# First batch of an attention and snake-MLP kernel: last keys in 1 KB rows on VectorE, three warm-up products fewer, two main products first, last division on GpSimd

## The chip, the cores and the metric

The kernel runs on one core of a Trainium2 chip. The metric is the device time of one execution in microseconds; the time of a kernel is the median of its runs. Engines are named as in the profile: PE is TensorE (PEld its weight loads), DVE is VectorE, ACT is ScalarE, POOL is GpSimd, and SP is the engine that issues most DMAs.

## The reference, cut to what matters

The first part is attention with pooled keys and values: batch 8, 8 heads, 576 tokens, head dimension 64. Keys and values are means over 8 neighbouring tokens, so that 72 keys are left.

```python
k_p = k.reshape(B, H, Sp, pool, D).mean(axis=3)        # pool 8, Sp 72
v_p = v.reshape(B, H, Sp, pool, D).mean(axis=3)
scores = scale * np.matmul(q, k_p.transpose(0, 1, 3, 2))
scores = scores - np.max(scores, axis=-1, keepdims=True)
attn = np.exp(scores)
attn = attn / (np.sum(attn, axis=-1, keepdims=True) + 1e-09)
out = np.matmul(attn, v_p)
```

Its output, 4608 tokens of 512 features, is the input of a second part, which is most of the work:

```python
h = x @ w_in                       # 512 -> 2048
s = np.sin(alpha * h)
g = h + s * s / (alpha + 1e-09)
y = g @ w_out                      # 2048 -> 512
```

All is float32.

## The kernel before

**Stages.** Tokens are worked on in nine units of 512 (`hidden(u, extra)`), each with four groups J of hidden features. A group's product is made by a scheme of the Strassen kind with seven products of half blocks, in the order 1, 5, 6, 2, 7, 3, 4. A unit thus has 28 slots, one product to a slot (L765, eight matmul records). The operands `as...` (combinations of blocks of `w_in`) are made by `combine_w_in` (L636); the operands `bt` (combinations of blocks of x) by `sums_of_x` (L738). After each product small pieces of work follow in the next slot: copies of partial sums on ScalarE (L791, L803, L805), sines and squares (L771, L778), additions on VectorE (L744, L832), a store of g to DRAM (L839). The second product of the MLP follows at the end (L1084); nothing in the change touches it.

**Attention beside it.** `carry(u)` writes out by hand in which slot of unit u the attention work for a later batch stands (`at(slot, f, ...)`). The order on every engine is the order in which the program issues the work; a DMA on SP likewise. So an instruction that waits holds back all that stands behind it on its engine.

**The first batch** has nothing to hide behind. `first_batch` runs it by pairs of heads: `load_k_heads` loads 512 of the 576 tokens' keys in rows of four tokens, adds them in two steps (L161, L163), and `k_head` sums pairs of rows by a matmul with `twos` (a matrix that adds neighbouring rows, L353) and copies the keys to `kb2` (L354). The last 64 tokens of all heads (8 keys each) are loaded by `load_k_rest` as 64 rows of 2 KB, added in three steps on GpSimd (L148) and transposed by `k_last` (L359, copied at L360). `q_head` transposes queries (L370, copied at L371). `products_head` multiplies the pair's queries with the keys (L391), and its keys include the last ones. `soft_shift` subtracts the maximum on VectorE (L397, L399), `soft_exp` takes the exponential on ScalarE (L405), `norm_head` sums (L411), takes the reciprocal (L412) and multiplies (L417). `a_head` transposes the attention weights of two pairs (L445, L453; copied at L447, L454), `values` multiplies them with pooled v (L533, L535), and `to_x` writes x (L504). Before k arrives, `warm` issues matmuls on the identity matrix, whose results nobody reads (L866). `refine` is a step that improves `c`, a square root (L605, L606).

Pairs 0 and 1 (heads 0 to 3) are finished in `first_batch`. Heads 4 to 7 go on in `carry(0)`: `a_head(1)` in slot 1, ahead of the second product of the slot order, `values` in slot 2, then the last 64 queries of batch 0: `rest_q` (L378, L379), `score(4)` (L320, L327, L328), `exp(4)` in slot 9, `norm_rest` in slot 20 (L423, L424, L428, L432, all on VectorE), `a_rest` in slot 23 (L460, L461, L462), `values_rest` in slot 24 (L546, L548).

Batch 1's attention runs in the same unit: `exp` and `norm` of four tiles (L336; sums L342, L343 on VectorE, multiplication L344 on GpSimd), `turn` (L470 and the lines after it), `move` (16 DMAs from `tr` to `aM`, L490), `all_values` in slot 26 (L563, L576; a one-element copy at L570, named `order`, reads the second bank in between), then `turn_q` (L210), which uses `tr` again. `load_v` of batch 1 sums v on GpSimd (L120), `load_k(2, e)` loads batch 2's keys in slot 16 (L108) and sums them there too (L120).

Of the kernel before, what the change touches and what calls it, by code (L numbers as in the profile page):

```python
# [13 lines left out]
F32 = mybir.dt.float32  # L14
AX = mybir.AxisListType.X
AF = mybir.ActivationFunctionType
OP = mybir.AluOpType
PSUM = bass.MemoryType.PSUM

P = 128  # L20
POOL = 8
# [19 lines left out]
class Kernel:  # L41
# [102 lines left out]
    def load_k_rest(self, x, out):  # L144

        D = self.D
        self.nc.sync.dma_start(out=x, in_=self.k[0, :, 4 * P:, :].rearrange("h (k t) d -> h k (t d)", t=POOL))
        add = lambda o, w, both=lambda y: y: self.nc.gpsimd.tensor_tensor(out=o, in0=both(x[:, 0:w]), in1=both(x[:, w:2 * w]), op=OP.add)  # L148
        add(x[:, 0:4 * D], 4 * D)
        add(x[:, 0:2 * D], 2 * D)  # L150
        add(out.rearrange("p (u d) -> p u d", u=2), D, lambda y: y.unsqueeze(1).to_broadcast([64, 2, D]))
        self.k_rest = out

# [75 lines left out]
    def attention(self, b):  # L229

        nc, D, H, Sp, NP, S = self.nc, self.D, self.H, self.Sp, self.NP, self.S
# [117 lines left out]
        def k_head(hp):  # L349

            ps = self.psum([P, 2, 64], 7 if hp % 2 else 0)
            for e in range(2):
                nc.tensor.matmul(ps[:, e], self.k_sums[:, 2 * hp + e].rearrange("p u d -> p (u d)"), self.twos[:], start=True, stop=True)  # L353
            nc.scalar.copy(out=self.kb2[:, 2 * hp:2 * hp + 2, 0:64], in_=ps)  # L354

        def k_last():

            ps = self.psum([P, H, Sp - 64], 4)
            nc.tensor.transpose(ps.rearrange("p h k -> p (h k)"), self.k_rest, self.ident[:64, :64])  # L359
            nc.scalar.copy(out=self.kb2[:, :, 64:Sp], in_=ps)  # L360
# [58 lines left out]
        def norm_rest():  # L419

            n = 64
            sm = self.sm.tile([P, H], F32, name="sm")
            nc.vector.tensor_reduce(out=sm[:n], in_=ex[:n, 5, :, 0:Sp + 1], axis=AX, op=OP.add)  # L423
            nc.vector.reciprocal(out=sm[:n], in_=sm[:n])  # L424
            for g in range(2):
                h = slice(4 * g, 4 * g + 4)
                m = sm[:n, h].rearrange("p (s e) -> p s e", s=2).unsqueeze(3).to_broadcast([n, 2, 2, 64])
                nc.vector.tensor_tensor(out=self.a4[:, 2 * g:2 * g + 2].rearrange("p e s k -> p s e k"),  # L428
                                        in0=ex[:n, 5, h, 0:64].rearrange("p (s e) k -> p s e k", s=2), in1=m, op=OP.mult)
            x = ex[:n, 5, :, 64:Sp].rearrange("p (hp e) k -> p hp e k", e=2)  # L430
            m = sm[:n].rearrange("p (hp e) -> p hp e", e=2).unsqueeze(3)
            nc.vector.tensor_tensor(out=self.z4[:, :, 0:2, :], in0=x, in1=m.to_broadcast([n, NP, 2, Sp - 64]), op=OP.mult)  # L432
# [120 lines left out]
        def all_values():  # L553
# [16 lines left out]
            nc.vector.tensor_copy(out=self.sm.tile([P, 1], F32, name="order")[:], in_=rest[:, 1, 0:1])  # L570
# [3 lines left out]
            for hp in hps:  # L574
                w, x = main[hp][1]
# [274 lines left out]
    def first_batch(self):  # L850
# [29 lines left out]
        self.load_k_rest(h[1][:64, 576:1088], far[1][:64, 1024:1152])  # L880
# [3 lines left out]
        for f in add_k[1:]:  # L884
            f()
        refine()
# [5 lines left out]
        warm(6, 3)  # L892
# [3 lines left out]
        A.q_head(1)  # L896
        A.products_head(0)
        A.k_head(1)
        A.soft_shift(0)
        A.q_head(2)  # L900
# [8 lines left out]
        A.norm_head(1, nc.gpsimd)  # L909
# [10 lines left out]
        A.norm_head(3, nc.vector)  # L920
# [10 lines left out]
    def carry(self, u):  # L931
# [5 lines left out]
        if u == 0:  # L937
            A0, A = self.att[:2]
            at(1, A0.a_head, 1, (5, 6, 7))
            at(1, self.half_k)  # L940
            at(2, A0.values, (2, 3), (2, 1))
            at(2, self.sums_of_x, 0, 1)
            at(2, A0.rest_q)
# [24 lines left out]
            at(20, A0.norm_rest)  # L968
# [9 lines left out]
            for e in range(2):  # L978
                at(16, self.load_k, 2, e)
# [348 lines left out]
```

## Time and profile before

| what | value |
|---|---|
| median of 4 runs | 923.27 us |
| the four runs | 919.65, 920.77, 925.77, 925.87 us |
| the profiled execution, its time | 920.77 us |
| its span in the profile | 919.0 us |
| its mean granted TensorE clock | 0.996 |
| TensorE busy from 0 to 6 us | 4.31 us |
| from 6 to 10 us | 2.95 of 4.00 us |
| from 10 to 15 us | 4.64 of 5.00 us |
| from 15 to 22 us | 6.18 of 7.00 us |
| from 22 to 60 us | 36.77 of 38.00 us |
| from 60 to 110 us | 48.18 of 50.00 us |
| first product L765 begins | 21.96 us |

How to read the profile: busy times are those of one execution, in microseconds from the span's start. A line such as L765 is a line of the kernel before. In a timeline a row is a run of like instructions: start, time, engine, line, operation, written tile and read tiles, count, and in brackets how long the engine stood idle before it and what it waited for. When several things were waited for, the one named is that which came last by the profile. The chain of waits follows what ended last back to the start.

### The profile page before, as it was taken

The page shows a single profiled execution, that of the slowest core. Times are in us where ns is not written, and L with a number is a line of the kernel's source. Part 1 is how long each engine was busy: PE and PEld are TensorE (multiplying, and loading weights), DVE is VectorE, ACT ScalarE, POOL GpSimd, SP SyncE. Part 2 cuts the span into 40 slices and gives each one's busy share as a digit, 9 for nine tenths or more (in the row PEclk, how much of TensorE's full clock was granted, in tenths as well). Part 3 has the DMA queues.
Part 4 walks back from the last instruction along what each step waited for, and adds up shares of the span by engine and source line. Part 5 has one row for each costly group of instructions (what it writes and reads, how often), then busy time and mean ns, then how long its engine had stood idle before and what let it go on. Part 6 is the DMA issues. An engine that isn't in the chain of part 4 may idle for free.

```text
span 919.0 us, 17718 instructions
## 1 busy us (share of the span) xinstructions
PE 903.3 (98%) x7006; PEld 819.9 (89%) x7006; DVE 670.9 (73%) x1005; ACT 435.8 (47%) x998; POOL 159.4 (17%) x155
## 2 busy tenths in 40 slices
PE   8999999999999999999999999999999999999997
PEld 6787887887878878888888899999999999999997
DVE  7666666746667566673466889988888888979894
ACT  5595685866757667586886631111111112111111
POOL 4593250612507034040000000000000000000000
PEclk9999999999999999999999999999999999999999
DMA  9984666766667556627327237171617253433401
GB/s 253 244 246 136 186 172 176 222 179 186 186 167 212 174 148 179 189 89 259 142 92 246 92 105 226 34 225 27 219 40 188 72 170 90 159 100 122 137 14 39
DMA packets 134666, 141.12 MB, mean 154 GB/s; under 512 B 49832, under 2 KB 103096, under 8 KB 134584
## 3 DMA queue, kind: packets, MB, share of 16 engines
q1 hardware_dynamic: 133240, 138.54, 52.1%
q10 hardware_dynamic: 1344, 1.45, 0.6%
q8 instruction: 55, 0.90, 0.4%
q14 instruction: 27, 0.22, 0.1%
HBM read 75.37 MB, written 47.19 MB: 133 GB/s over the span
## 4 chain that ended last, share of the span: by engine, by line
PE 90%; DMA 3%; POOL 2%; SPq 2%; DVE 1%; issue 1%; ACT 0%; POOLq 0%; ACTq 0%
PE PS L765 44%; PE PS L1084 41%; PE PS L287 2%; PE PS L563 2%; DMA a<-in_moe_w_in_dram 2%; SPq L630 1%; DMA kvin<-in_v_dram 1%; PE PS L576 1%; POOL as L636 1%; DMA home<-in_k_dram 1%; POOL ex L344 0%; POOL kvin L120 0%; DVE last L428 0%; SPq L96 0%; POOL a L636 0%
## 5 line engine op out<-in xcount | busy, mean ns | idle before, releaser
L765 PE MATMUL PS<-home,a 128*128 128x256 f32 x1152 | 264.3, 381 | 0.8 <-ACT home L504 0.5
L765 PEld LDWEIGHTS PS<-home,a 128*128 128x128 f32 x1152 | 216.5, 190 | 37.0 <-issue 4.5
L765 PE MATMUL PS<-home,as 128*128 128x256 f32 x864 | 202.7, 384 | 0.5 <-issue 0.5
L765 PEld LDWEIGHTS PS<-home,as 128*128 128x128 f32 x864 | 164.2, 192 | 24.6 <-issue 1.7
L1084 PE MATMUL PS<-s,wb 128*128 128x144 f32 x896 | 119.3, 286 | 0.4 <-ACT PS L1197 0.4
L1084 PEld LDWEIGHTS PS<-s,wb 128*128 128x128 f32 x896 | 113.7, 190 | 0.7 <-ACT PS L1197 0.6
L778 ACT ACTIVATE s<-s,c 128x256 f32<-128x256 f32 (+1 forms) x216 | 110.0, 572 | 0.0
L744 DVE TENSOR_TENSOR h<-PS,p 128x512 f32<-128x512 f32 x72 | 49.2, 684 | 79.3 <-PE PS L765 47.5
L120 POOL TENSOR_TENSOR kvin<-kvin 96x768 f32<-96x768 f32 (+3 forms) x40 | 66.3, 1659 | 194.5 <-DMA kvin<-in_v_dram 189.4
L771 ACT ACTIVATE s<-h,al 128x256 f32<-128x256 f32 x144 | 65.1, 503 | 56.1 <-DVE h L744 55.2
L1197 ACT COPY PS<-PS 128x144 f32<-128x144 f32 x56 | 14.7, 263 | 145.7 <-PE PS L1084 144.3
L771 ACT ACTIVATE s<-PS,al 128x256 f32<-128x256 f32 x144 | 59.9, 467 | 37.0 <-PE PS L765 17.4
L1084 PE MATMUL PS<-r,wb 128*128 128x144 f32 x512 | 73.2, 286 | 0.0
L1084 PE MATMUL PS<-s,a 128*128 128x144 f32 x512 | 73.2, 286 | 0.0
L832 DVE TENSOR_TENSOR h<-PS,s 128x512 f32<-128x512 f32 x36 | 24.7, 685 | 58.4 <-ACT s L778 58.4
L1084 PEld LDWEIGHTS PS<-r,wb 128*128 128x128 f32 x512 | 67.1, 190 | 0.1
L1084 PEld LDWEIGHTS PS<-s,a 128*128 128x128 f32 x512 | 67.1, 190 | 0.0
L1216 ACT COPY PS<-PS 128x144 f32<-128x144 f32 x56 | 14.7, 263 | 88.5 <-PE PS L1084 88.5
L1084 PE MATMUL PS<-s,we 128*128 128x144 f32 x384 | 54.9, 286 | 0.0
L1084 PE MATMUL PS<-x,wb 128*128 128x144 f32 x384 | 54.9, 286 | 0.0
L1084 PEld LDWEIGHTS PS<-s,we 128*128 128x128 f32 x384 | 50.4, 190 | 0.1
L832 DVE TENSOR_TENSOR h<-h,s 128x1024 f32<-128x1024 f32 x36 | 50.4, 1400 | 0.0
(185 smaller groups left out, 1191.8 us busy)
## 6 DMA issues: line engine op xcount, KB each, us to landing
g_bridge<-h SPq DMA_DIRECT2D x72, 512.0 KB
r<-g_bridge SPq DMA_DIRECT2D x31, 1152.0 KB
out_dram<-o SPq DMA_DIRECT2D x128, 72.0 KB
kvin<-in_k_dram SPq DMA_DIRECT2D x14, 576.0 KB
q<-in_q_dram SPq DMA_DIRECT2D x7, 1024.0 KB
kvin<-in_v_dram SPq DMA_DIRECT2D x14, 512.0 KB
aM<-tr SPq DMA_DIRECT2D x56, 92.0 KB
aM<-tr SPq DMA_DIRECT2D x56, 88.0 KB
```

The costliest lines, as they stand in the source:

```text
L120: self.nc.gpsimd.tensor_tensor(out=t[..., 0:w] if w > D else out, in0=t[..., 0:w], in1=t[..., w:2 * w], op=OP.add)
L287: nc.tensor.matmul(ps[e][r0 + r:r0 + r + q.shape[-1], h, :], q[s], kb[s, hp, :], start=True, stop=True)
L563: nc.tensor.matmul(o[r:r + 64], w, x, start=start and i < 2, stop=False, skip_group_check=True)
L576: nc.tensor.matmul(ps[hp], w.rearrange("p e d -> p (e d)"), x, start=False, stop=True, skip_group_check=True)
L744: add = lambda o, x, y: nc.vector.tensor_tensor(out=o, in0=x, in1=y, op=OP.add)
L765: nc.tensor.matmul(ps[:, jj, :], self.A[p][:, kk, f * P:(f + 1) * P], x[:, kk, :], start=(start and jj == 0 and kk == 0), stop=(kk == 1), ...
L771: nc.scalar.activation(out=G.s[:, i, jj, j, :], in_=src[:, jj], func=AF.Sin, scale=self.al[:, f:f + 1])
L778: nc.scalar.activation(out=x, in_=x, func=AF.Square, scale=self.c[:, f:f + 1])
L832: add = lambda o, x, y: self.nc.vector.tensor_tensor(out=o, in0=x, in1=y, op=OP.add)
L1084: nc.tensor.matmul(out, W[:, J // 2, J % 2, :], A[:, J, :], start=(start and J == 0), stop=(J == self.NJ - 1), skip_group_check=True)
L1197: nc.scalar.copy(out=x1[:, 0, :], in_=x0[:, 1, :])
L1216: nc.scalar.copy(out=x1[:, 1, :], in_=x1[:, 0, :])
```

## The change

Nine edits, all in the work of the first batch or in unit 0:

- `load_k_rest` loads the last keys as 128 rows of 1 KB (four tokens each) and no longer as 64 of 2 KB; its additions are two, on VectorE, and are issued by a function that it returns. `k_last` then sums pairs of rows by a matmul with `twos` where it transposed.
- The copy of the first pair's keys to `kb2` and that of the last keys go from ScalarE to VectorE.
- `warm(6, 3)` becomes `warm(3, 3)`.
- The additions of pairs 1 to 3's keys are issued after `k_last`; `q_head(1)` after `k_head(1)`; `refine` after the first `soft_shift`.
- `norm_head(1)` multiplies on VectorE, `norm_head(3)` on GpSimd, each the other way before.
- In `carry(0)`, `a_head(1)` goes from slot 1 to slot 2, behind `rest_q`, which itself goes to the head of slot 2; so the second product comes ahead of both.
- `norm_rest` goes from slot 20 to slot 17 and multiplies on GpSimd.
- `order` of batch 1 goes from VectorE to ScalarE.
- `load_k(2, e)` goes from slot 16 to slot 17.

```diff
-        self.nc.sync.dma_start(out=x, in_=self.k[0, :, 4 * P:, :].rearrange("h (k t) d -> h k (t d)", t=POOL))
-        add = lambda o, w, both=lambda y: y: self.nc.gpsimd.tensor_tensor(out=o, in0=both(x[:, 0:w]), in1=both(x[:, w:2 * w]), op=OP.add)
-        add(x[:, 0:4 * D], 4 * D)
-        add(x[:, 0:2 * D], 2 * D)
-        add(out.rearrange("p (u d) -> p u d", u=2), D, lambda y: y.unsqueeze(1).to_broadcast([64, 2, D]))
+        self.nc.sync.dma_start(out=x, in_=self.k[0, :, 4 * P:, :].rearrange("h (r t) d -> h r (t d)", t=4))
         self.k_rest = out
+
+        def add():
+            self.nc.vector.tensor_tensor(out=x[:, 0:2 * D], in0=x[:, 0:2 * D], in1=x[:, 2 * D:4 * D], op=OP.add)
+            both = lambda y: y.unsqueeze(1).to_broadcast([P, 2, D])
+            self.nc.vector.tensor_tensor(out=out.rearrange("p (u d) -> p u d", u=2), in0=both(x[:, 0:D]), in1=both(x[:, D:2 * D]), op=OP.add)
+        return add
...
-            nc.scalar.copy(out=self.kb2[:, 2 * hp:2 * hp + 2, 0:64], in_=ps)
+            (nc.scalar.copy if hp else nc.vector.tensor_copy)(out=self.kb2[:, 2 * hp:2 * hp + 2, 0:64], in_=ps)
...
-            nc.tensor.transpose(ps.rearrange("p h k -> p (h k)"), self.k_rest, self.ident[:64, :64])
-            nc.scalar.copy(out=self.kb2[:, :, 64:Sp], in_=ps)
+            nc.tensor.matmul(ps.rearrange("p h k -> p (h k)"), self.k_rest, self.twos[:], start=True, stop=True)
+            nc.vector.tensor_copy(out=self.kb2[:, :, 64:Sp], in_=ps)
...
-                nc.vector.tensor_tensor(out=self.a4[:, 2 * g:2 * g + 2].rearrange("p e s k -> p s e k"),
+                nc.gpsimd.tensor_tensor(out=self.a4[:, 2 * g:2 * g + 2].rearrange("p e s k -> p s e k"),
...
-            nc.vector.tensor_tensor(out=self.z4[:, :, 0:2, :], in0=x, in1=m.to_broadcast([n, NP, 2, Sp - 64]), op=OP.mult)
+            nc.gpsimd.tensor_tensor(out=self.z4[:, :, 0:2, :], in0=x, in1=m.to_broadcast([n, NP, 2, Sp - 64]), op=OP.mult)
...
-            nc.vector.tensor_copy(out=self.sm.tile([P, 1], F32, name="order")[:], in_=rest[:, 1, 0:1])
+            (nc.vector.tensor_copy if b > 1 else nc.scalar.copy)(out=self.sm.tile([P, 1], F32, name="order")[:], in_=rest[:, 1, 0:1])
...
-        self.load_k_rest(h[1][:64, 576:1088], far[1][:64, 1024:1152])
+        add_rest = self.load_k_rest(h[1][:, 576:832], far[1][:, 1024:1152])
...
-        for f in add_k[1:]:
-            f()
-        refine()
+        add_rest()
...
-        warm(6, 3)
+        warm(3, 3)
         A.k_head(0)
         A.q_head(0)
         A.k_last()
-        A.q_head(1)
+        for f in add_k[1:]:
+            f()
         A.products_head(0)
         A.k_head(1)
+        A.q_head(1)
         A.soft_shift(0)
+        refine()
...
-        A.norm_head(1, nc.gpsimd)
+        A.norm_head(1, nc.vector)
...
-        A.norm_head(3, nc.vector)
+        A.norm_head(3, nc.gpsimd)
...
-            at(1, A0.a_head, 1, (5, 6, 7))
-            at(1, self.half_k)
+            at(2, A0.rest_q)
+            at(2, A0.a_head, 1, (5, 6, 7))
+            at(2, self.half_k)
             at(2, A0.values, (2, 3), (2, 1))
             at(2, self.sums_of_x, 0, 1)
-            at(2, A0.rest_q)
...
-            at(20, A0.norm_rest)
+            at(17, A0.norm_rest)
...
-                at(16, self.load_k, 2, e)
+                at(17, self.load_k, 2, e)
```

On every engine the number of instructions stays nearly the same: TensorE has three warm-up matmuls fewer, ScalarE one copy fewer, GpSimd three additions fewer and three multiplications more.

## The prediction

> **What bounds the kernel now.** I read the page first (busy shares and the chain of waits), then granted clock by stretch, then the timeline around the edits.
>
> ```profile
> PE 903.3 (98%) x7006; PEld 819.9 (89%) x7006; DVE 670.9 (73%) x1005; ACT 435.8 (47%) x998; POOL 159.4 (17%) x155
> ...
> PE 90%; DMA 3%; POOL 2%; SPq 2%; DVE 1%; issue 1%; ACT 0%; POOLq 0%; ACTq 0%
> ```
>
> TensorE is the bound: it is busy for 98% of the span, and it does not lose work (three warm-up products apart). So the change can only win what TensorE loses in the first 90 us, which is all that it touches. Busy time by stretch from 0 to 110 us adds up to 103.0 of 110, so 7 us of idle time, and the clock adds to it:
>
> ```profile
> 27.00:30.50 3.50, 2.46 (x17) 0.75 (x17) 2.99 (x2) 1.35 (x3) 3.34 (x5) 1.00 1.15 230
> 30.50:34.00 3.50, 3.50 (x22) 2.91 (x23) 2.74 (x7) 2.32 (x5) 0.21 (x1) 0.53 1.11 344
> 75.00:78.30 3.30, 2.11 (x11) 1.31 (x10) 3.30 (x5) 2.05 (x5) 2.35 (x3) 1.00 0.63 148
> 78.30:81.70 3.40, 3.40 (x28) 2.25 (x26) 1.02 (x1) 0.66 (x3) 0.00 (x0) 0.53 0.63 148
> ```
>
> Columns: stretch, its length, busy time of TensorE, its weight loads, VectorE, ScalarE and GpSimd, granted clock, DMA share, GB/s. Each half-clock stretch follows one in which TensorE idled for over a microsecond. Eight matmuls of L765 take 3.27 and 3.18 us there and 1.9 us elsewhere, so such a stretch costs up to half its 3.4 us, 1.7 us.
>
> The first idle time is the wait of L320 for `q_rest`'s copy (1.0 us), which stands on ScalarE behind L504. The second is the division of the last tokens:
>
> ```profile
> 68.79 0.71 DVE L470 STREAM_TRANSPOSE tr<-ex 128x512 f32<-128x512 f32 x1 [1.15 <-POOL ex L344]
> 69.43 0.27 DVE L473 STREAM_TRANSPOSE tr<-ex 128x128 f32<-128x128 f32 x1
> 69.62 0.65 DVE L744 TENSOR_TENSOR h<-PS,p 128x512 f32<-128x512 f32 x1
> ...
> 70.33 3.32 PEld L765 LDWEIGHTS PS<-home,a 128*128 128x128 f32 x16 [0.17 <-DVE h L744]
> ...
> 72.95 0.74 DVE L423 TENSOR_REDUCE sm<-ex 64x8 f32<-64x584 f32 x1
> ...
> 73.84 2.94 POOL L120 TENSOR_TENSOR kvin<-kvin 96x768 f32<-96x768 f32 x2
> 73.95 3.10 DVE L428 TENSOR_TENSOR last<-ex,sm 64x256 f32<-64x256 f32 x2
> ...
> 77.12 0.34 PE L460 MATMUL PS<-ident,last 64*128 64x64 f32 x2 [0.80 <-DVE last L428]
> ```
>
> Two things are to be seen. The divisions L428 take 1.55 us each, for half the elements of the 128x512 addition L744 at 0.65 us: they run only as GpSimd's L120 lets them. And TensorE at 70.33 waits for L744, which stands on VectorE behind a transpose that waits for GpSimd's L344. GpSimd's work before it runs nearly without a gap from 46.63, when v of batch 1 has landed. So TensorE has a gate at 70.3 whose time comes from DMA and GpSimd: what is gained before it is lost there.
>
> **What the Trainium skill says.** "TensorE: Matmul & The Clock Gate", section "What's actually happening": an activity monitor gates TensorE to half clock after an idle window of about 3.4 us. The trace agrees in size (0.53 in both stretches), but here a window two thirds busy was enough. "GPSIMD Engine Reference", section "Specifications": GpSimd shares its SBUF interfaces with VectorE, and instructions of VectorE with two SBUF inputs contend. L428 agrees: 1.55 us each beside L120. The same page, "Performance versus the Vector engine": elementwise work is about twice as slow on GpSimd. It agrees: L161 128x256 takes 0.74 us on POOL and 0.39 us on DVE.
>
> **The change part by part.**
>
> *Last keys.* Removed: three L148 on POOL (0.72 + 0.59 + 0.52 = 1.83 us, from 6.51 to 8.50), which L359 waited for (1.1 us), and two ScalarE copies (0.27 + 0.21). Added on VectorE: two 128x128 additions, not in the trace as such; bounds 0.17 us each (L605, 128x16) and 0.42 us (L163, 128x256); I take 0.55 us for both, and 0.45 us for two PSUM copies (ScalarE's took 0.27 and 0.21). Same 128 KB and place in SP's queue, so I keep the landing at 6.5 us; 1 KB rows instead of 2 KB ones may move it by 0.3 us either way. The last keys are then transposed near 7.1 instead of 8.55 and the first L391 starts near 7.65 instead of 9.34. Behind the waiting addition on VectorE stand the copy of keys 0 and 1 and the sums of keys 2 and 3 (landed 7.16, now 7.57): k_head(1) runs at about 8.6, not 10.0. But q_head(1) now follows it, and the second L391 needs that copy: about 10.45 instead of 11.03. Of 1.7 us, 0.6 is left. GpSimd's sums of keys 4 to 7 gain at most 0.27 us, since L161 waits for DMA already.
>
> *Warm-ups.* Three of six matmuls (half of 2.93 us) go. k_head(0) starts when its sums are ready (4.99) instead of 6.0; nothing follows from it, since the last keys come at 7.1. Bounds: 0, or 1.7 us lost on a chain with slack if the clock falls.
>
> *Order on VectorE.* `refine` (four L605/L606: 0.17 to 0.58 us each, 0.9 to 1.4 in all) goes behind the first soft_shift, ahead of the second, and its products of two SBUF tiles meet GpSimd's sums. The second shift starts at about 11.6 (11.9 before). Division 1 moves to VectorE (L417 there: 0.97 us for both parts) and division 3 to GpSimd (1.29 us). So a_head(0) may start near 15.95 (16.86), but shift 2 waits for the division: 16.1 (15.14), and shift 3 ends near 19.4 (18.29). ScalarE's queue passes this on:
>
> ```profile
> 18.51 0.70 ACT L405 ACTIVATE ex<-ex 128x576 f32<-128x576 f32 x1
> ...
> 19.09 0.57 ACT L454 COPY aM<-PS 64x512 f32<-64x512 f32 x1
> ...
> 20.36 1.13 PE L535 MATMUL PS<-aM,vz 32*128 32x512 f32 x4
> ```
>
> Exponential 3 stands ahead of the copy L454 that L535 needs. Later by 1.1 us, it puts the first main product at about 22.6 instead of 21.95: 0.65 us lost; bounds 0.9 gained to 1 lost.
>
> *Second main product first.* Before, from the start F of the first L765: a_head(1) to F+3.2, second product to F+5.0, values to F+7.1, the last tokens' queries, the wait, scores to F+9.6, third product at F+9.55. After: two products to F+3.9, queries 4.3, a_head(1) 5.9, values 8.35 (their copies are no longer covered by the product: 0.2), scores 9.1, while two L504 (1.08) and L738 (0.69) still stand before the third product: F+10.25. It loses 0.7 us, wins the L320 wait, and leaves about 1.2 us idle elsewhere. If the half clock after it goes, 1.7 us come back. So TensorE comes out between 1.7 us earlier and 1.4 us later. To the gate at 70.3 an earlier arrival counts nothing.
>
> *Division of the last tokens.* L423 and L424 (0.74 + 0.19) now stand between L473 and L744, so the gate opens at 71.3: 0.95 us lost. GpSimd does L428 and L432 behind L344: 0.55 + 0.55 + 0.26 by L417's rate there, from 70.65 to 72.05. L460 needs them at 76.8: hidden, with 4.7 us of cover. Gone are the waits around L460 (between products it took TensorE 2.07 us, from 75.78 to 77.85; without waits about 0.6, as the four like transposes of L378 took 0.46: 1.45 us) and probably the half clock behind them (1.7). TensorE reaches all_values at about 83.55 instead of 85.75. There the next comes late: the aM moves of L490 (16 issues, 10.1 us on SP) start after the last transpose, now 72.6 instead of 71.8, and their landing, 83.4 before by VectorE's wait in L210, becomes 84.2. So some 1.6 us are kept, 2.2 at best. k of batch 2 is issued behind a store (2.26 us of SP, 10 us later), summed 1.7 us later and needed at 91: covered. `order` on ScalarE (0.16 us) keeps TensorE from L210's queue, which now ends near 87.4.
>
> **Sum.** -1.45 -1.7 +0.95 of the division gives -2.2, of which late moves leave -1.6; the front adds 0, since up to 0.9 us of delay hides in the later gate. The profiled execution (span 919.0, 920.77 around it) would go to 919.2; on the median of four runs (923.27) it is **921.6**.
>
> **Rivals.** *Larger gain:* the gate itself opens earlier. GpSimd's additions are stretched where VectorE reads two SBUF tiles (one L636 2.30 us instead of 1.27, another 1.92); shifted in time they may lose up to 2 us, and with 2.2 kept the gain is 4.2: 919. Against it: GpSimd starts from the same landing of v.
>
> *Slower:* the half clock comes back after the new stall. The idle 0.95 us at 70.4 and the 1.2 us before the third product fill a window as the old waits did. One more half-clock stretch (1.7), with the old ones kept and 0.5 us of front delay beyond the gate, gives +2.2: 925.5. It decides once a window drops to about two thirds busy; for it speaks that such windows were throttled twice, against it that 6 to 10 us, with 2.95 of 4.00 busy, was not.
>
> *Nothing:* the aM moves land as late as the gain is large: 923.3.
>
> **Chances.** Forecast 0.48, larger gain 0.2, slower 0.24, nothing 0.08. The four runs shown lie from 919.65 to 925.87, and this spread comes on top of every case: range 917.3 to 926.0. One per cent is 9.2 us, about what a measurement here tells from no change; all idle and half-clock time of the front is 10 us, so faster by more has 0.03; slower by more would need five more half-clock stretches: 0.03.
>
> **What would show it.** Right: VectorE's divisions gone near 74 to 77.6, L460 without wait, a wait of about 1 us for L744's line near 70.4, full clock from 78 to 82, a first main product at 22 to 23. Wrong: a third half-clock stretch, TensorE waiting near 84 for far longer than 1 us, or a first L391 not before 9.

## The result, and the profile after

| what | before | after |
|---|---|---|
| median of all runs | 919.71 us (56 runs, 914.50 to 930.67) | 919.84 us (35 runs, 915.64 to 927.83) |
| ratio after to before | | 1.0004, 95% interval 0.9991 to 1.0018 |
| profiled execution, its time | 920.77 us | 921.34 us |
| its span | 919.0 us | 919.5 us |
| its mean granted clock | 0.996 | 0.998 |

No difference can be measured: the interval reaches from 0.8 us faster to 1.7 us slower. The ratio is taken from the fast runs alone, without the few that lie more than 1.5% above their kernel's fastest, and so it is not the quotient of the two medians. From L148 on, line numbers of after are those of before plus two for what the text speaks of (L765 is L767, L391 is L393, L490 is L492); in e3a and e7 it is plus four, in e9 and e10 plus two.

The page, its busy shares and the end of its chain of waits:

```profile
PE 902.6 (98%) x7001; PEld 819.8 (89%) x7001; DVE 666.2 (72%) x1005; ACT 435.4 (47%) x997; POOL 162.2 (18%) x155
...
PE 94%; DVE 2%; DMA 1%; issue 1%; SPq 1%; ACT 0%; POOL 0%; ACTq 0%; DVEq 0%; POOLq 0%
```

TensorE is still the bound. The same four stretches as in the prediction, now of after, with the same columns:

```profile
27.00:30.50 3.50, 3.50 (x26) 2.02 (x25) 2.08 (x2) 1.54 (x3) 3.42 (x4) 1.00 1.05 283
30.50:34.00 3.50, 2.25 (x24) 1.29 (x21) 2.86 (x5) 2.66 (x6) 1.25 (x4) 1.00 0.91 297
75.00:78.30 3.30, 3.30 (x19) 2.58 (x17) 1.10 (x2) 2.47 (x6) 3.14 (x3) 1.00 0.73 154
78.30:81.70 3.40, 3.40 (x37) 2.76 (x36) 0.72 (x1) 1.85 (x7) 3.32 (x3) 1.00 0.57 134
```

Both half-clock stretches are gone (clock 1.00 in the second and fourth row, 0.53 before), and so is the idle time at 75 us. New is idle time from 30.5 to 34: 1.25 us. But the second half-clock stretch isn't always there in before either. A second profile of the same kernel, c0_before, waits 0.67 us at L460 and then runs the next product at full clock (1.99 us; 3.18 us in the first profile):

```profile
77.78 1.99 PE L765 MATMUL PS<-home,as 128*128 128x256 f32 x8
```

So of the prediction's 1.7 us for that stretch, one of two profiles of before had nothing to give back. The timeline of after from 66 to 92 us shows where the division's gain went:

```profile
67.11 2.82 POOL L346 TENSOR_TENSOR ex<-ex,sm 128x576 f32<-128x576 f32 x2 [2.13 <-DVE sm L345]
...
70.05 0.69 DVE L746 TENSOR_TENSOR h<-PS,p 128x512 f32<-128x512 f32 x1
...
70.89 3.62 PE L767 MATMUL PS<-home,a 128*128 128x256 f32 x16
...
72.06 11.18 SPq L492 DMA_DIRECT2D aM<-tr  x16
...
76.17 0.46 PE L462 MATMUL PS<-ident,last 64*128 64x64 f32 x4
...
84.94 0.65 PE L565 MATMUL PS<-aM,vm 64*64 64x512 f32 x6 [1.90 <-DMA aM<-tr]
...
88.58 1.99 PE L767 MATMUL PS<-home,as 128*128 128x256 f32 x8
```

L462 runs without a wait, but TensorE then stands for 1.90 us at L565, for the moves into `aM`, which SP took 11.18 us to issue. The product behind all_values starts at 88.58; before it was 89.17. Of the 1.6 us that the prediction kept, 0.6 were there.

Those too are lost afterwards, in code that both kernels have alike. Busy times from 110 to 200 us (TensorE, weight loads, VectorE, ScalarE, GpSimd, then the clock), first of before, then of after:

```profile
110.00:200.00 90.00, 90.00 (x642) 75.68 (x640) 58.30 (x101) 65.36 (x136) 33.58 (x31) 1.00 0.64 184
```

```profile
110.00:200.00 90.00, 87.77 (x605) 74.37 (x607) 57.03 (x98) 63.29 (x130) 35.52 (x32) 0.98 0.61 176
```

TensorE was busy for all of it before and for 87.77 us after, at a clock of 0.98. The timeline of after names the place, the score matmuls of unit 2:

```profile
158.42 0.85 PE L289 MATMUL PS<-kblk,q 64*64 64x72 f32 x39
161.50 1.61 PE L289 MATMUL PS<-kblk,q 64*64 64x72 f32 x57 [2.23 <-issue]
163.04 2.97 PE L767 MATMUL PS<-home,as 128*128 128x256 f32 x8
```

39 of 96 small matmuls, then 2.23 us in which TensorE waited for nothing that the profile shows ("issue"), and half clock behind it: eight matmuls of L767 took 2.97 us instead of 1.99. The trace's list of DMA packets has one of 16 KB on the instruction queue at 158.80, which took 1.18 us. The run has 55 of them. TensorE has by far the most instructions, 14,002 (7001 matmuls and as many weight loads), so these packets are taken to be its own, at some 255 instructions each; this is an inference from the count.

### The profile page after: what moved, and what is told of

The parts are those of the page before. It is cut to its first block, busy times and chain, and to the rows that moved or that the text cites. A ratio compares the mean times of both kernels' runs of the same rounds, so it can differ in the third digit from the quotient of the medians.

```text
span 919.5 us, 17704 instructions
## 1 busy us (share of the span) xinstructions
PE 902.6 (98%) x7001; PEld 819.8 (89%) x7001; DVE 666.2 (72%) x1005; ACT 435.4 (47%) x997; POOL 162.2 (18%) x155
## 3 DMA queue, kind: packets, MB, share of 16 engines
q10 hardware_dynamic: 1344, 1.45, 0.6%
## 4 chain that ended last, share of the span: by engine, by line
PE 94%; DVE 2%; DMA 1%; issue 1%; SPq 1%; ACT 0%; POOL 0%; ACTq 0%; DVEq 0%; POOLq 0%
PE PS L767 45%; PE PS L1087 41%; PE PS L289 2%; PE PS L565 2%; DMA kvin<-in_k_dram 1%; PE PS L578 1%; SPq L492 0%; PE PS L868 0%; PE PS L535 0%; PE PS L372 0%; PE PS L537 0%; PE PS L262 0%; PE PS L251 0%; DMA aM<-tr 0%; DVE h L834 0%
## 5 line engine op out<-in xcount | busy, mean ns | idle before, releaser
L767 PE MATMUL PS<-home,a 128*128 128x256 f32 x1152 | 264.3, 381 | 0.8 <-ACT home L506 0.5
L767 PEld LDWEIGHTS PS<-home,a 128*128 128x128 f32 x1152 | 216.5, 190 | 37.1 <-issue 5.0
L767 PE MATMUL PS<-home,as 128*128 128x256 f32 x864 | 201.2, 382 | 1.7 <-DVE home L740 1.2
L767 PEld LDWEIGHTS PS<-home,as 128*128 128x128 f32 x864 | 163.4, 191 | 25.7 <-DVE home L740 1.8
L746 DVE TENSOR_TENSOR h<-PS,p 128x512 f32<-128x512 f32 x72 | 49.2, 684 | 80.3 <-PE PS L767 46.9
L120 POOL TENSOR_TENSOR kvin<-kvin 96x768 f32<-96x768 f32 (+3 forms) x40 | 66.4, 1660 | 186.3 <-DMA kvin<-in_v_dram 180.9
L1087 PEld LDWEIGHTS PS<-x,wb 128*128 128x128 f32 x384 | 50.3, 190 | 0.0
```

Of the source, the lines that this page charges most:

```text
L120: self.nc.gpsimd.tensor_tensor(out=t[..., 0:w] if w > D else out, in0=t[..., 0:w], in1=t[..., w:2 * w], op=OP.add)
L746: add = lambda o, x, y: nc.vector.tensor_tensor(out=o, in0=x, in1=y, op=OP.add)
L767: nc.tensor.matmul(ps[:, jj, :], self.A[p][:, kk, f * P:(f + 1) * P], x[:, kk, :], start=(start and jj == 0 and kk == 0), stop=(kk == 1), ...
L1087: nc.tensor.matmul(out, W[:, J // 2, J % 2, :], A[:, J, :], start=(start and J == 0), stop=(J == self.NJ - 1), skip_group_check=True)
```

## The experiments

Landmarks of each profiled execution, in us. "Clock" is where the trace first records full clock; keys 2 to 4 are the first transposes of the keys of batches 2 to 4 (L249 before); "2 to 4" is the time between, in which all kernels run the same code; "tail" is from keys 4 to the start of the last row of matmuls. "First product" and "third" are in the order of time; the "moves" are the 16 DMAs into `aM`, for which all_values waits; the "gate" is the wait of slot 20's product for L744.

| kernel | clock | first product | third | L460 | keys 2 | 2 to 4 | tail | ratio to before, interval |
|---|---|---|---|---|---|---|---|---|
| before | 6.81 | 21.96 | 31.50 | 75.98 | 91.16 | 110.6 | 710.7 | |
| c0_before | 7.72 | 21.43 | 31.46 | 76.04 | 90.81 | 109.5 | 709.6 | |
| after | 11.46 | 22.86 | 33.20 | 76.17 | 90.57 | 113.5 | 709.0 | 1.0004 (0.9991 to 1.0018) |
| e1_rest_only | 7.00 | 21.26 | 31.33 | 75.96 | 89.28 | 114.0 | 709.9 | 1.0004 (0.9984 to 1.0024) |
| e2_front_only | 12.55 | 23.32 | 34.08 | 77.04 | 91.38 | 113.5 | 709.6 | 1.0038 (1.0018 to 1.0058) |
| e3a_k_dma16 | 11.47 | 23.17 | 33.77 | 76.73 | 90.05 | 114.1 | 709.2 | 1.0011 (0.9995 to 1.0027) |
| e3_rest_slot15 | 11.79 | 23.13 | 33.48 | 77.01 | 90.54 | 113.5 | 710.5 | 1.0010 (0.9992 to 1.0027) |
| e4_warm6 | 7.26 | 22.56 | 33.55 | 78.20 | 91.92 | 109.5 | 711.6 | 1.0003 (0.9976 to 1.0030) |
| e5_norm_swap_back | 12.69 | 23.00 | 40.42 | 84.78 | 98.65 | 109.5 | 706.8 | one run, 923.24 us |
| e6_second_late | 7.07 | 22.04 | 31.42 | 76.37 | 90.41 | 109.9 | 707.9 | one run, 916.48 us |
| e7_queues | 12.68 | 23.38 | 34.12 | 77.09 | 89.30 | 109.5 | 709.8 | 0.9998 (0.9978 to 1.0019) |
| e8_slots | 5.07 | 21.68 | 31.48 | 79.34 | 93.29 | 109.5 | 710.2 | 1.0017 (0.9998 to 1.0036) |
| e9_slots_queues | 7.06 | 21.32 | 31.12 | 78.47 | 90.67 | 109.5 | 712.4 | 0.9998 (0.9970 to 1.0026) |
| e10_rest_queues | 8.11 | 21.42 | 30.62 | 74.52 | 86.73 | 110.4 | 709.4 | 0.9987 (0.9963 to 1.0011) |

The tail spreads over 5.6 us and "2 to 4" over 4.7, in the same code. A median that is to show 2 us stands against this; the landmarks up to keys 2 are what tells the parts apart.

### The last-token part alone: e1_rest_only

The kernel before with the division on GpSimd in slot 17, `order` on ScalarE and `load_k(2, e)` in slot 17. The edit, cut:

```diff
-                nc.vector.tensor_tensor(out=self.a4[:, 2 * g:2 * g + 2].rearrange("p e s k -> p e s k"),
+                nc.gpsimd.tensor_tensor(out=self.a4[:, 2 * g:2 * g + 2].rearrange("p e s k -> p e s k"),
...
-            at(20, A0.norm_rest)
+            at(17, A0.norm_rest)
```

> The kernel before with the last tokens' part of the change alone (norm_rest in slot 17 on GpSimd, order on ScalarE, load_k(2) in slot 17). Theory 'moves' (the division's gain is real and is mostly given back at all_values, where the aM moves land late): L460's transposes run without a wait, no half clock at 78 to 82, TensorE waits 1 to 2 us for aM at 83 to 85, and the product behind all_values starts at 88.3 to 88.9 (89.17 before, 88.58 after). Time 0.3 to 1 us under before. Theory 'front' (the front's delay is what cost the gain): without it that product starts at 87.7 or earlier and the time is 1.5 us or more under before. Theory 'noise' (half-clock stretches and instruction fetches decide): the same start as in the changed kernel, time within 1 us of before.

Keys 2 came at 89.28, 1.9 us ahead of before; the moves took 10.10 us to issue, and 0.82 us of waiting for them was left. The product behind all_values started at 87.28, where "front" had it (87.7 or earlier) and a microsecond ahead of "moves". The last-token part works as a step. The time shows none of it (ratio 1.0004), and can hardly tell the theories apart: its interval reaches from 1.5 us less to 2.2 us more. The profiled execution lost 4.4 us more than c0_before in "2 to 4".

### The front alone: e2_front_only

The kernel after with the five lines of the last-token part as before. The edit, cut to one of them:

```diff
-            at(17, A0.norm_rest)
+            at(20, A0.norm_rest)
```

> The changed kernel without the last tokens' part: only the front's edits. Theory 'moves': the front gives nothing by itself; the first main product starts at 22.9 and the third at 33.2 as in the changed kernel (21.96 and 31.5 before), TensorE reaches slot 20 some 0.5 us late or not at all, L460 waits for the divisions as before, and the time is 0 to 1 us over before. Theory 'front': 1 us or more over before. Theory 'noise': within 1 us of before whatever the starts.

The front was measured as a loss: ratio 1.0038, the only interval of all that leaves out 1. That one of ten such intervals does so by chance is not rare, and after, with the same front, has 1.0004. First product 1.4 us later than before, third product 2.6, slot 20's product 1.4 (71.77 against 70.40), slot 23's L460 1.1, keys 2 0.2 us later. VectorE's L430 still took 3.03 us for two, and TensorE waited 0.18 us for it. How so small a delay at keys 2 would make 3.5 us at the end isn't seen in this one execution, so the loss in time is not explained and may be chance.

### Who makes the moves late: e3a_k_dma16, e3_rest_slot15

One issues batch 2's key loads in slot 16 and their sums in 17, the other the division in slot 15 and keys in 16. The edits (of the first one, the branch of `load_k` that hands back the sums is left out):

```diff
-            for e in range(2):
-                at(17, self.load_k, 2, e)
+            sums = []
+            for e in range(2):
+                at(16, lambda e=e: sums.append(self.load_k(2, e, 2)))
+                at(17, lambda e=e: sums[e]())
```

> The changed kernel with the DMAs of batch 2's keys issued in slot 16 again (their sums stay in slot 17 behind the divisions). Theory 'moves by the load' (this load, moved in front of the moves, slows them): SP issues the 16 moves in 10.1 us instead of 11.2, the wait at all_values falls from 1.9 to about 0.8 us, and the product behind it starts at 87.5 instead of 88.58; time about 1 us under the changed kernel. Theory 'moves by the start' (they are late because VectorE's last sums stand ahead of the last transpose): wait and start stay within 0.2 us of the changed kernel.

```diff
-            at(17, A0.norm_rest)
+            at(15, A0.norm_rest)
...
-                at(17, self.load_k, 2, e)
+                at(16, self.load_k, 2, e)
```

> The changed kernel with norm_rest in slot 15 (its sums in VectorE's idle time before 64 us, its multiplications in GpSimd's before 67) and the load of batch 2's keys in slot 16 with its sums. Theory 'moves' in either form: the moves start about 0.9 us earlier (71.1 instead of 72.06) and are issued in 10.1 us, so the wait at all_values is 0 to 0.3 us and the product behind it starts at 86.6 to 86.9; time 1.5 to 2 us under the changed kernel. Theory 'noise': the start moves, the time stays within 1 us.

In e3a the moves were issued from 72.61 in 10.09 us, with a wait of 0.81 us; in e3 from 73.10 (later, not earlier) in 10.10 us, with 1.03 us. In e3 the sums of v started at 46.50, 1.5 us later than in after, so it is no clean test of an earlier division. So 11.18 us is one execution's figure, load_k's place is not the cause (e1 has it in slot 17 and 10.10 us), and a wait of 0.8 to 1.9 us stays whatever stands beside it.

### Is the stall at 159 us the change's? c0_before

The kernel before, unchanged, a second time.

> The kernel before, looked at once more: is the stretch from 155 to 165 us of its one profile typical? Every changed kernel profiled so far has a stall of TensorE of 2.3 to 2.7 us near 159 us, inside the score matmuls of unit 2 (L289), and half clock for some 3.4 us after it; the profile of the kernel before has none there. Theory 'chance': the stall comes with the fetch of TensorE's instructions, not with the change; it is to be seen here too, a 16 KB packet of the instruction queue beside it, kp(3) still at 146.2 and kp(4) at 203.5 to 204.5 instead of 201.7. Theory 'change': no stall there, kp(4) at 201.7 +-0.3, and the 2 us that the changed kernels lose after 150 us are a cost of the change.

By itself this spoke for "change": no stall, "2 to 4" 109.5 us. But e4, e5, e6 and e7, which all hold the change's front and division, have none either (109.5 to 109.9). The same block in c0_before, whole:

```profile
158.71 1.67 PE L287 MATMUL PS<-kblk,q 64*64 64x72 f32 x96
```

There the instruction packets came at 147.28 and 162.26, outside the block. In after, e1, e2, e3a and e3 one came at about 158 to 159.5, in it. It was also late there: 27 to 28 us behind the packet before it, where the nine others have 16 to 20 us. So these 4 us go with the time of a fetch, not with an edit; that the late fetch is what stops TensorE is inferred from this. What makes it late these runs don't show. A rival is the chip: e1, e2, e3a and e3 were profiled on one chip and all have the stall, the other eight experiments on three other chips and none has it. Against it stands that the medians of before, which ran beside them, are 919.07 us on that chip and 918.71 to 920.00 on the others.

### Warm-ups: e4_warm6

```diff
-        warm(3, 3)
+        warm(6, 3)
```

> The kernel after with six warm-up matmuls again (three more). Theory 'clock': the three missing warm-ups keep TensorE at half clock to 11.5 us, and this delays the front. Then full clock from about 6.8 to 7.5, the second L393 at 10.5 (after: 11.61; the prediction's 10.45), the first main product L767 at 21.8 (after: 22.86), the third product at 32.1 (33.20), and the time 0.5 to 1.2 us below that of after. Theory 'no matter' (the prediction's value for the warm-ups, 0): second L393 at 11.5 and first main product at 22.8 as in after. Theory 'gate': the front moves as in 'clock', but from 70 us on every landmark lies within 0.3 us of after's (product of slot 20 at 70.8, kp(2) at 90.6) and the time is the same.

Full clock from 7.26, but the second L393 only at 11.32: k_head(0) now waits behind the warm-ups (6.21 instead of 5.05), and VectorE's addition for pair 1 met GpSimd's (L165 0.98 us instead of 0.42). "Clock" got the clock right and its worth wrong. The third product was even later than in after (33.55), since VectorE's addition before it took 1.33 us (after: 0.69). The first product came at 22.56, 0.3 us ahead of after. Ratio 1.0003: no gain.

The rest of the answer comes from e6, whose front is that of after to the instruction up to 22 us. Timeline of e6_second_late, then of after:

```profile
7.70 0.73 PE L393 MATMUL PS<-h,q 64*64 64x72 f32 x32 [0.42 <-ACT q L373]
...
10.16 0.73 PE L393 MATMUL PS<-h,q 64*64 64x72 f32 x32 [0.24 <-ACT q L373]
```

```profile
7.79 1.24 PE L393 MATMUL PS<-h,q 64*64 64x72 f32 x32 [0.41 <-ACT q L373]
...
11.61 0.73 PE L393 MATMUL PS<-h,q 64*64 64x72 f32 x32
```

The same 32 matmuls take 0.73 or 1.24 us, and the eight of L372 between the two rows 1.04 or 1.82 us. With three warm-ups full clock came at 11.5 to 12.7 in six executions of seven and at 7.07 in one; with six it came at 5.07 to 8.11 in all seven. It is chance with odds that the warm-ups shift, and it is worth 1.45 us at the second L393 and 0.82 us at the first product (22.04 against 22.86). The Trainium skill ("TensorE: Matmul & The Clock Gate", section "What's actually happening") says that the monitor's window runs freely, so that the clock rises at a time that differs from run to run, by 500 ns either way. The case agrees that it differs, but by far more: 5.6 us between executions with three warm-ups (7.07 to 12.69), 3.0 us with six.

### Divisions 1 and 3: e5_norm_swap_back

```diff
-        A.norm_head(1, nc.vector)
+        A.norm_head(1, nc.gpsimd)
...
-        A.norm_head(3, nc.gpsimd)
+        A.norm_head(3, nc.vector)
```

> The kernel after with the divisions of pairs 1 and 3 on their engines of before (pair 1 on GpSimd, pair 3 on VectorE). The prediction's step: division 1 on VectorE (1.08 us) stands ahead of shift 2 and so makes shift 3, exponential 3, the copy L456 and the first main product later by about 0.65 us. Then here shift 2 starts at 15.8 (after: 16.76), L456 at 19.9 to 20.0 (20.61) and the first main product at 22.2 (22.86). Rival: the late clock alone makes the front late, and GpSimd, which then does pairs 0 and 1 one after the other, holds up a_head(0): L447 at 17.5 or later instead of 17.02, first main product at 22.8 to 23.1.

The rival's times came true at the front: L447 at 17.91, first product at 23.00. It is no clean test of the prediction's step, since the clock rose at 12.69 here and at 11.46 in after, which put the fourth L393 0.5 us later. Even so shift 2 started at 16.18 (after: 16.76) and L456 at 20.15 (20.61): division 1 on VectorE does hold these up. TensorE met that delay in another place than the prediction had it. Timeline of after:

```profile
18.64 0.60 PE L455 MATMUL PS<-ident,tr 128*64 128x128 f32 x4 [0.54 <-DVE vz L183]
```

L183 (`vz`, pooled v with a mask) stands on VectorE behind shift 2. L537, which needs L456, ran without a wait. In e5 that wait is gone, but L447 waited for GpSimd's division (0.29 us) and started 0.9 us later. Then came something that neither had. Timeline of e5:

```profile
25.90 3.51 DVE L740 TENSOR_TENSOR home<-home 128x512 f32<-128x512 f32 x1
26.39 1.25 POOL L638 TENSOR_TENSOR a<-a,a 128x512 f32<-128x512 f32 x1
27.61 1.26 POOL L638 TENSOR_TENSOR as<-a,as 128x512 f32<-128x512 f32 x1
29.47 3.53 PE L767 MATMUL PS<-home,as 128*128 128x256 f32 x8 [4.47 <-DVE home L740]
```

VectorE's L740, the operand of the second product, took 3.51 us instead of 0.69 to 1.10: it ended half a microsecond after GpSimd's second L638 was through (28.87). The Trainium skill ("GPSIMD Engine Reference", section "Specifications") has a cause that fits: the two engines share SBUF interfaces, and VectorE's instructions with two SBUF inputs contend. The trace shows the overlap. In after GpSimd did division 3 first and came to L120 at 24.88, when L740 was done. In e5 it was at L120 from 21.71, and VectorE's work ahead of L740 was stretched as well. The place of the divisions isn't enough for this: before has them on the same engines, but there the keys of batch 1 landed later, L120 started at 23.93, behind this addition, and it took 0.69 us. TensorE was idle for 4.47 us in e5; this isn't in the prediction.

### Second product ahead: e6_second_late

```diff
-            at(2, A0.rest_q)
-            at(2, A0.a_head, 1, (5, 6, 7))
-            at(2, self.half_k)
+            at(1, A0.a_head, 1, (5, 6, 7))
+            at(1, self.half_k)
             at(2, A0.values, (2, 3), (2, 1))
             at(2, self.sums_of_x, 0, 1)
+            at(2, A0.rest_q)
```

> The kernel after with the order of before in slots 1 and 2: a_head(1) ahead of the second product, the last queries behind values. The prediction's step: second product first wins the wait of L322 (about 1.0 us) and the half clock behind it (1.7 us), and loses 0.7 us on the third product's start. Then here: first main product as in after (22.9), a wait of 1.0 us at L322, third product near 32.4 (F + 9.5; after: 33.20), half clock again for 3.4 us from about 31.6, and the product behind the third at 35.5 (after: 35.04). Rival: the half clock doesn't come back (the window holds more work than before's), then third product 32.4 and the next at 34.3, and the change of order is a loss of 0.7 us. In both, kp(2) within 0.4 us of after's 90.57, if the waits near 83 us cover what is gained.

```profile
27.00:31.00 4.00, 2.96 (x29) 1.25 (x30) 2.44 (x2) 1.35 (x3) 3.44 (x5) 1.00 1.10 326
31.00:34.40 3.40, 3.40 (x17) 2.72 (x14) 2.82 (x6) 2.70 (x5) 2.07 (x2) 0.50 1.10 348
```

From its first product (22.04) the third starts 9.4 us later and the next at 34.70, 12.7 us later; in after it is 10.3 and 12.2 (35.04). The half clock came back (0.50). So the new order is worth half a microsecond by the fourth product: it trades a half-clock stretch for 1.25 us of idle time, as the prediction had it. Where that stretch doesn't come, the new order loses: e10, with the old order and full clock, has the third product 9.2 us and the fourth 11.0 us from the first, 1.1 us sooner than after.

### Moves on two queues: e7_queues

Half of the 16 moves are issued by GpSimd, its sums of batch 2's keys behind them (that part of the edit is left out).

```diff
-                        nc.sync.dma_start(out=self.aM[r:r + 32, a, 0:w], in_=tr[32 * a:32 * a + 32, c, s, 0:w])
+                        (nc.gpsimd if c and b == 1 else nc.sync).dma_start(out=self.aM[r:r + 32, a, 0:w], in_=tr[32 * a:32 * a + 32, c, s, 0:w])
```

> The kernel after; 8 of the 16 moves into aM of batch 1 are issued by GpSimd and no longer by SP, and for that GpSimd's sums of batch 2's keys are issued behind them (slot 20 instead of 17). Theory 'moves': what was kept of the division's gain was small (0.6 us at 90 us instead of the predicted 1.6) because the 16 issues on one queue take 10 to 11 us and the last lands near 84.8, when TensorE has been waiting for 1.9 us (from 82.7). With two queues SP's share ends near 77, the wait at L565 falls below 0.3 us, the product behind all_values starts at 86.6 to 87.0 (after: 88.58) and kp(2) at 88.7 to 89.1 (90.57). Rival 'GpSimd issues slowly': its eight issues take 1.2 us each or more, the last lands at 84 or later, wait and kp(2) as in after within 0.4 us. Rival 'next wait': the moves land early, but L565 then waits for something else (the copies of the banks, sums of k that are now late), kp(2) not below 90. Of the whole time: at most 1.8 us less than after, which is inside what a median of this many runs tells from none.

Timeline of e7_queues:

```profile
72.96 7.49 SPq L494 DMA_DIRECT2D aM<-tr  x8
...
73.16 4.10 POOL L494 DMA_DIRECT2D aM<-tr  x8 [0.67 <-DVE tr L484]
...
83.89 0.65 PE L567 MATMUL PS<-aM,vm 64*64 64x512 f32 x6
...
87.30 1.99 PE L769 MATMUL PS<-home,as 128*128 128x256 f32 x8
```

The wait is gone, although the front of this execution was 0.9 us later than that of after (L460 at 77.09): product behind all_values at 87.30 (after: 88.58), keys 2 at 89.30 (90.57); both miss the foretold times by 0.2 to 0.3 us, less than that delay. GpSimd's eight issues took 4.10 us; SP's eight still took 7.49, so they ended at 80.5 and not near 77. That the issue on one queue makes the moves late (theory "moves") is shown for the landmarks up to keys 2; in the time it doesn't show (ratio 0.9998).

### Another order in slots 1 and 2, and both: e8_slots, e9_slots_queues

On e1: the last queries first in slot 1, `half_k` and the last queries' scores behind the operands of the third and later products; e9 adds the two queues.

```diff
+            at(1, A0.rest_q)
             at(1, A0.a_head, 1, (5, 6, 7))
-            at(1, self.half_k)
...
             at(2, self.sums_of_x, 0, 1)
-            at(2, A0.rest_q)
-            at(2, A0.score, 4)
+            at(2, self.half_k)
             at(2, self.sums_of_x, 0, 2)
             at(2, self.sums_of_x, 0, 3)
+            at(2, A0.score, 4)
```

> The kernel before with the last-token part of the change alone (as in e1_rest_only), and another order in slots 1 and 2: the last queries first in slot 1, ahead of a_head(1); the reduction L113 and the last queries' maxima behind the addition L738 that the third product waits for. Theory 'front order': of e1's stretch 28.3 to 31.3 the wait of L320 (1.05 us) goes, because the copy L379 stands ahead of L504 on ScalarE, and the third product waits for L738 alone, which starts when L504 ends (29.4 + 0.4): third product at 30.4 to 30.7 (e1: 31.33), idle time of TensorE 1.0 to 1.3 us in place of 1.9, and no half clock behind it (e1: from 30.9, 1.5 us); the fourth product 2.3 us earlier than in e1. Rival 'window': the remaining idle time still brings half clock, then the third product's eight matmuls take 3.3 us and only 0.7 us is won. In both, theory 'gate' holds that at 90 us no more than 0.5 us of it is left (e1: kp(2) 89.28), since the moves wait for work that starts with the landing of v.

> e8_slots and the moves on two queues of e7_queues together. Theory 'two limits': the front's gain passes the gate at 70 us only if the moves don't hold it: product of slot 20 at 69.0 to 70.0, no wait at all_values above 0.4 us, kp(2) at 86.5 to 88.0 (before: 91.16; e1: 89.28), so 3 to 4.5 us ahead of before there, and the time 1 to 4 us below before's if no stall of instruction fetch or half clock takes it back. Rival: TensorE is held at 70 us by the work behind the landing of v; kp(2) at 88.5 to 89.5 and the time as e1's.

A miss. L320's wait and the half clock at 31 went, and the fourth product came at 33.31 (e1: 34.61). Two microseconds on, a new wait took more. Timeline of e8:

```profile
34.11 1.55 DVE L738 TENSOR_TENSOR home<-home 128x512 f32<-128x512 f32 x1
35.59 1.75 DVE L738 TENSOR_TENSOR home<-home,home 128x512 f32<-128x512 f32 x1
...
38.33 0.63 PE L260 MATMUL PS<-ident,q 128*128 128x128 f32 x4 [2.70 <-DVE ex L328]
```

The transposes L260 wait for L328, which this order puts behind two L738, and these took 1.55 and 1.75 us beside GpSimd. Half clock followed at 39.2 (e9: 37.8). In e8 1.46 us of waiting for the moves followed at all_values. In e9 the two queues took that out again, but of the front's loss nothing came back: keys 2 at 90.67 where 86.5 to 88.0 was expected.

### Without the front: e10_rest_queues

> The kernel before with the last-token part of the change (as in e1_rest_only) and the moves on two queues (as in e7_queues); nothing of the change's front. Theory 'two terms': the last-token part takes the waits around L460 and the half clock behind them out, and the second queue the wait at all_values that then comes up (e1: 0.82 us, from 82.8). Where e1 has the product behind all_values at 87.28 and kp(2) at 89.28, this kernel has them at 86.0 to 86.4 and 88.0 to 88.4, so some 3 us ahead of before (91.16), and half clock near 31 as before and e1. Its time, against before's: 1 to 3 us less, ratio 0.997 to 0.999, if the fetches of TensorE's instructions in units 2 to 5 take no more than they do in before on average. Rival: kp(2) as foretold, but the ratio's interval holds 1: what a run loses to those fetches and the clock differs by more from one execution to the next than these 3 us.

Keys 2 came at 86.73, 4.4 us ahead of before and more than expected: no half clock came at 31, although TensorE waited 1.05 us at L322. In before and e6, with 1.04 us there and no second wait, it came (e1 and c0_before had a second wait of 0.8 us behind it). Its median is 916.52 us of 14 runs, with 918.71 of 19 for before beside it: the lowest of the kernels with several runs, but the ratio's interval, 0.9963 to 1.0011, holds 1. It also shows the gate of the prediction:

```profile
44.52 3.71 POOL L122 TENSOR_TENSOR kvin<-kvin 128x1024 f32<-128x1024 f32 x2 [6.76 <-DMA kvin<-in_v_dram]
...
65.47 2.73 POOL L346 TENSOR_TENSOR ex<-ex,sm 128x576 f32<-128x576 f32 x2
...
68.40 0.69 DVE L746 TENSOR_TENSOR h<-PS,p 128x512 f32<-128x512 f32 x1
...
69.14 3.07 PE L767 MATMUL PS<-home,a 128*128 128x256 f32 x13 [0.74 <-DVE h L746]
```

GpSimd runs on without a wait from v's landing, and TensorE waits for L746, as before at 70.33. But v is 2.1 us earlier than in before (44.52 against 46.63), and the gate 1.3 us (69.14 against 70.40), with the last tokens' sums already ahead of L746. From v to the gate it is 24.62 us here and 23.77 in before: 0.85 us more, near the 0.95 that the prediction put on these sums.

## Why the prediction was right, and where not

The call, no measurable difference, was right. The change of -1.6 us that it forecast was not there: the ratio's interval ends at -0.8 us. That the measured 919.84 us lies in the range is partly luck: the median it started from was 3.6 us too high, and the range was 8.7 us wide. Step by step:

- **Last keys: right but for the clock.** Two additions took 0.58 us (0.55), two copies 0.50 (0.45), the first L393 started at 7.79 (7.65). The second came at 11.61 instead of 10.45. The term that failed is the warm-ups', of whose bounds, "0, or 1.7 us lost on a chain with slack if the clock falls", the sum took 0: TensorE stayed at half clock to 11.46, and e6, with the clock from 7.07, has that L393 at 10.16. The bound of 1.7 us holds the measured 1.45; the chain had little slack, for 0.82 us of it were left at the first product.
- **Order on VectorE: first product 22.86 (22.6), by other reasons.** `refine` took 1.16 us, inside the bounds. The late clock, which isn't in this sum, is worth 0.82 us (e6, with the clock early: 22.04). With that clock the step comes out at 0.1 us and not at 0.65. Division 1 does hold up VectorE, but not by way of exponential 3 and L454 (L456 in after): TensorE waited 0.54 us at L455, for L183. Back on GpSimd (e5) the first product was no earlier, with a clock that rose still later; what the division's place alone is worth stays open. That the number came out near is luck.
- **Second product first: right.** Third product at F + 10.3 (F + 10.25), a wait of 1.25 us (1.2), no half clock there. The bounds in its last sentences don't add up, though: 0.65 later for the first product, 0.7 lost and 1.7 won make 0.35 earlier to 1.35 later, not 1.7 to 1.4.
- **Gate at 70.3: mechanism right, place wrong.** In after TensorE didn't wait there; it arrived half a microsecond later by itself (70.89 against 70.40), and GpSimd stood for 2.13 us waiting for VectorE. In c0_before TensorE didn't wait there either (70.77). The first profile of before had the latest landing of v of all. "GpSimd starts from the same landing of v" was the false sentence: it started between 43.6 and 46.6 us in the fourteen executions. So no 0.95 us was lost at the gate in after (where the gate does hold, e10 shows 0.85), and "up to 0.9 us of delay hides in the later gate" failed too: in e2 all of the first product's delay of 1.4 us was still there at slot 20.
- **Waits of L460 and half clock gone: the waits right, the half clock a sample.** TensorE reached all_values at 83.0 (83.55 foreseen). c0_before has the waits and no half clock, and reached it at 84.1 where before did at 85.75. So the 1.7 us belong to one of two executions of before. In the reading of L428, "half the elements" of L744 is so per partition; in all it is a quarter (64x256 against 128x512).
- **Moves: the mechanism right, the size wrong.** The landing came at 84.8 (84.2), and 0.6 us was kept instead of 1.6. This is the rival "Nothing" in the main. e7 shows it: issue on two queues, and the wait is gone. Of the error of 1.0 us, 0.6 is the later landing (84.8 for 84.2), of which SP's 11.18 us, one execution's figure, made 1.1 against an earlier start of 0.5; the rest lies between the landing and the product.
- **load_k(2): covered, as said** (e3a).
- **The rival "half clock comes back":** neither new wait, 1.25 us at 33 and 1.90 us at 83, brought it in after. The first did in e4, where it was 1.88 us.
- **The level.** 921.6 us stood on the median of four runs, 923.27; over 56 runs it is 919.71. Against that the forecast change would have given 918.1.

## What to carry to other kernels

A wait that is taken away in one place has a next wait behind it: before pricing the gain, look for the transfer that the freed engine will meet next, and count how long one queue needs to issue it. A wait that stands in one profile alone, such as a gate that follows from a landing, is a sample; a second profile of the same kernel tells whether it is there. Here it would have shown neither the gate's wait nor the second half-clock stretch. Where VectorE adds two SBUF tiles, look at what GpSimd does at that moment: an addition took 1.09 us in after and 3.51 in e5, where two divisions had changed places and GpSimd was at other work.

## What the runs showed of the hardware

- A block of 96 small matmuls (L289, 1.67 us) stood for 2.2 to 2.6 us in the five executions in which a 16 KB packet, taken to be TensorE's instructions, arrived in it, late; half clock followed for 3.4 us in all five. The profile shows "issue" and no wait. 55 packets serve the whole run. In the same code ("2 to 4") these five executions of fourteen took 4.0 to 4.7 us longer than the shortest.
- Half clock behind a wait is not certain: with a wait of 1.04 to 1.05 us near 30 us it came in before and e6 and not in e10; behind the waits at L460 it came in before and not in c0_before.
- One VectorE addition of two SBUF tiles of 128x512 (the operand of the second product) took from 0.69 us to 3.51 us; the longest ran beside GpSimd's L120 and L638.
- Eight DMA issues took 4.10 us on GpSimd and 7.49 us on SP, in the same stretch of e7 (4.09 and 7.15 us in e10).
